# Reordering the passes of the last stage of a backward kernel, and thinning one DMA queue before it

## The chip, the cores and the metric

The kernel runs on one core of one Trainium2 chip. The metric is the device time of one execution in microseconds (us); the profile's span is the part of it that the hardware profiler records.

## What is computed

The reference is the forward pass and the whole backward pass of a block with sequence length S = 2048, width D = 576, H = 32 heads of 128 and a hidden width F = 4608, in bf16:

```python
xn = _layernorm(x, axis=-1)
s = _A_ref(xn, A_k_cache, A_v_cache, A_wq, A_wo)   # attention over the given K and V, projected by wo
g = _silu(_B_ref(xn, B_w_gate, B_w_up, B_w_down))  # (sigmoid(xn Wg) * (xn Wu)) Wd
return x + s * g
...
_out, _vjp = jax.vjp(_f, A_x, A_k_cache, A_v_cache, A_wq, A_wo, B_w_gate, B_w_up, B_w_down)
_grads = _vjp(grad_out)
```

There are nine outputs: the result and eight gradients. What matters here is the gradient of the normalised input, dxn = du Wu^T + dg Wg^T + dQ Wq^T, from which the layernorm's backward pass makes dx (`out_1`), and the gradients dK and dV (`out_2`, `out_3`).

## The kernel before

The kernel goes through stages one after the other: layernorm with the gate and up products, the down product, the attention heads one by one (about two thirds of the time), the output product, the gradients of the hidden layer, then the two stages that matter here. Intermediates that don't fit on the chip go to DRAM and come back: du and dg (`du_d`, `dg_d`, 2048 x 4608), dQ (`dq2_d`) and the heads' outputs (`on2_d`), both 2048 x 4096.

**Turns.** For 23 of the heads dK and dV are computed transposed and lie in `dkT_d` and `dvT_d`. The helper `turn` (L152 to L160) brings one such tile back with a transposing DMA (L157) and, on its next call, stores the tile that the call before has loaded (L160). Each of the 46 turns is 0.5 MB in and 0.5 MB out. Calls are strewn over the last three stages. Each stage has two buffers for them.

**The dW_o and dW_q stage** (L990 to L1056) runs over NHG = 8 groups of 4 heads. A group forms 4 products for dW_o (L1025) and then the products for dW_q (L1036, L1045) from two loaded tiles, `onb` and `dqb` (L1011, L1012), each double buffered. Along the way groups load W_u^T and W_g^T, transposed by the DMA, into `wuT_sb` and `wgT_sb` (L1054). A group calls `turn` twice: behind its first product (L1028) and at its end (L1055). A last call after the loop only stores (L1056).

**The last stage** (L1058 to L1122) runs over NSB = 8 blocks of 256 rows. A block has eight passes that all add to the same four accumulators (two tiles of 128 rows, each split into 512 and 64 columns): three over du with `wuT_sb`, three over dg with `wgT_sb`, each 12 hidden tiles of 128 deep, and two over dQ with `wqT`, each 16 tiles deep. A pass first loads its chunk of du, dg or dQ by a transposing DMA (L1083), 128 x 12 x 256 or 128 x 16 x 256 elements, into one of three buffers (`cf0` to `cf2`) or one of two (`cq0`, `cq1`); a buffer can be loaded anew only when the pass that reads it has ended. W_q^T comes in four quarters of five transposing DMAs each (L92), issued behind the loads of passes 1, 3, 4 and 6 of block 0. The first dQ pass needs quarters 0 and 1, the second quarters 2 and 3. Blocks 1 to 6 call `turn` behind the loads of passes 1 and 5. After its last pass a block's accumulators are drained by ScalarE (L1102), VectorE does the layernorm's backward pass (L1107 to L1119), and dx is stored (L1120).

**What sets the order.** Every DMA with `nc.sync` is issued by SyncE (SP), which keeps the order of the program text (the `manual_schedule` of both stages lists SP). So a load waits until everything ahead of it in SP's queue has been issued, and an entry that waits for a buffer or for a landing holds up all entries behind it. The tiles of the last stage lie where the dW_o stage's tiles were: `cf0` where the dQ tile of even groups was (last used by group 6), `cf2` partly where that of the last group was.

Of the kernel before, what the change touches and what calls it, by code (L numbers as in the profile page):

```python
# [9 lines left out]
bf = mybir.dt.bfloat16  # L10
f32 = mybir.dt.float32
PSUM = bass.MemoryType.PSUM
DRAM = bass.MemoryType.DRAM
P = 128
# [81 lines left out]
def kernel(  # L96
# [6 lines left out]
    nc = tc.nc  # L103
    cfg = dict(cfg or {})
    _, S, D = A_x.shape
    _, H, Sk, Dh = A_k_cache.shape
# [4 lines left out]
    FT = F // P  # L111
    dts = ktiles(D)
    DT = len(dts)
    ncs = ktiles(D, 512)
# [37 lines left out]
    def turn(pool, load=True):  # L152
        old, turned[:] = list(turned), []
        if load and turns:
            src, dst = turns.pop(0)
            t_ = pool.tile([P, NT, P], bf, name="turn")
            nc.sync.dma_start_transpose(t_[:], src)  # L157
            turned.append((dst, t_[:]))
        for (dst, t_) in old:
            nc.sync.dma_start(dst, t_)  # L160
# [30 lines left out]
    with tc.tile_pool(name="pa", bufs=1) as pa:  # L191
# [159 lines left out]
        if True:  # L351
# [9 lines left out]
            with tc.tile_pool(name="a2h", bufs=1, reuse_waits="tile") as hp, \  # L361
# [12 lines left out]
                for sg in range(NT // SG):  # L374
# [7 lines left out]
                    for sl in range(SG):  # L382
# [426 lines left out]
    if True:  # L809
# [19 lines left out]
        with tc.tile_pool(name="c1b", bufs=1, side="right", reuse_waits="tile") as blk, \  # L829
# [29 lines left out]
            for st in range(NT):  # L859
# [9 lines left out]
                accs = [ps.tile([P, 512], f32, name=f"acc{j}") for j in range(len(ncs))]  # L869
# [119 lines left out]
        NHG = H // HG  # L989
        with tc.tile_pool(name="c2b", bufs=1, reuse_waits="tile") as blk, tc.tile_pool(name="c2s", bufs=2, reuse_waits="tile") as sb, \  # L990
# [26 lines left out]
            for hg in range(NHG):  # L1017
                cols = slice(hg * HG * P, (hg + 1) * HG * P)
                onb, dqb = held.pop(hg)
                for hl in range(HG):  # L1020
                    h = hg * HG + hl
                    accs = [ps.tile([P, 512], f32, name=f"acc{j}") for j in range(len(ncs))]
                    for st in range(NT):
                        for j, (n0, nn) in enumerate(ncs):
                            nc.tensor.matmul(accs[j][:, :nn], lhsT=onb[:, st, hl * P:(hl + 1) * P], rhs=ds_all[:, st, n0:n0 + nn],  # L1025
                                             start=(st == 0), stop=(st == NT - 1))
                    if hl == 0:
                        turn(tkp)  # L1028
# [23 lines left out]
                load_hg(hg + 2)  # L1052
                for (dst, src, d0, kd) in wT_loads[2 * hg:2 * hg + 2]:
                    nc.sync.dma_start_transpose(dst[:, :, d0:d0 + kd], src[d0:d0 + kd, :])  # L1054
                turn(tkp)  # L1055
            turn(tkp, False)  # L1056

        SB2 = min(256, S)  # L1058
        FC = ldiv(FT, 12)
        HC = ldiv(H, 16)  # L1060
        with tc.tile_pool(name="c4c", bufs=1, reuse_waits="tile") as chp, tc.tile_pool(name="c4s", bufs=2, reuse_waits="tile") as sb, \
# [11 lines left out]
            for sbi in range(S // SB2):  # L1073
                scol = slice(sbi * SB2, (sbi + 1) * SB2)
                nsl = SB2 // P
                accs = [[ps.tile([P, 512], f32, name=f"acc{sl}_{j}") for j in range(len(ncs))] for sl in range(nsl)]
                passes = []
                for (src_d, wT, nK, KC, nm) in ((du_d, wuT_sb, FT, FC, "cu"), (dg_d, wgT_sb, FT, FC, "cg"), (dq2_d, None, H, HC, "cq")):
                    for k0 in range(0, nK, KC):
                        passes.append((src_d, wT, k0, KC, nm))  # L1080
                for pi, (src_d, wT, k0, KC, nm) in enumerate(passes):
                    ch = chp.tile([P, KC, SB2], bf, name=f"cq{pi % 2}" if nm == "cq" else f"cf{pi % 3}")
                    nc.sync.dma_start_transpose(ch[:], src_d[scol, k0 * P:(k0 + KC) * P])  # L1083
                    if sbi == 0 and pi in (1, 3, 4, 6):
                        load_wqT((1, 3, 4, 6).index(pi))
                    elif sbi and sbi < NSB - 1 and pi % 4 == 1:
                        turn(tkp)
                    last = pi == len(passes) - 1
                    for kk, sl in ([(kk, sl) for sl in range(nsl) for kk in range(KC)] if last else
                                   [(kk, sl) for kk in range(KC) for sl in range(nsl)]):  # L1090
                        k_ = k0 + kk
                        w_ = wT[:, k_, :] if wT is not None else wqT_q[k_ // HQ][:, k_ % HQ, :]
                        for j, (n0, nn) in enumerate(ncs):
                            nc.tensor.matmul(accs[sl][j][:, :nn], lhsT=ch[:, kk, sl * P:(sl + 1) * P], rhs=w_[:, n0:n0 + nn],  # L1094
                                             start=(pi == 0 and kk == 0), stop=(last and kk == KC - 1))
                for sl in range(nsl):
                    st = sbi * nsl + sl
                    rows = slice(st * P, (st + 1) * P)
# [19 lines left out]
                    dx = sb.tile([P, D], bf, name="dx")  # L1118
                    nc.vector.tensor_tensor(dx[:], t2[:], got[:], op=ALU.add)  # L1119
                    (nc.sync if sbi == NSB - 1 else nc.gpsimd).dma_start(o1[rows, :], dx[:])  # L1120
            turn(tkp, False)
            assert not turns  # L1122
        pc3.release()
# [31 lines left out]
```

## Time and profile before

| what | us |
|---|---|
| median of three runs | 5089.01 |
| lowest and highest of them | 5059.81, 5113.86 |
| the profiled execution | 5071.54 |
| its span | 5069.6 |
| TensorE (PE) busy in it | 4957.5 |
| SP's waits for PE in the last stage (L1083 for L1094), 35 times | 106.0 |
| PE's waits at L1094 for loads of `cf` and `cq`, all in block 0 | 9.4, 7.1 and 1.4 |

In a timeline a line gives the start and the duration in us, the engine, the line of code, the operation, the tiles (written <- read) and how many instructions were merged; brackets give the idle time of the engine before them and what ended it. SPq lines show the time that SP took to issue a DMA, not the transfer. In a table of stretches the last columns are the granted PE clock (1.00 is full), the busy share of the DMA engines (overlapping packets make it exceed 1) and the GB/s moved. DMA landing times are counted from the start of the issue.

### The profile page before, as it was taken

Reading aid. Unit: us, or ns where it says so; the run is one execution under the profiler, and the core shown is the slowest. Engines: PE = TensorE matmul, PEld = TensorE weight load, DVE = VectorE, ACT = ScalarE, POOL = GpSimd, SP = SyncE. Lnnn points to the kernel's source line nnn. Section 1 sums busy time; section 2 is a strip of 40 time slices with the busy share of each in tenths; the row PEclk is TensorE's granted clock in tenths of the full one; section 3 lists DMA queues with packets and bytes.
Section 4 is the critical chain, followed back from the end, with each engine's and each line's share of the span. In section 5 each row is a group of like instructions: output and inputs, shape, how many; then the busy total and the mean of one; then the engine's idle time right before and its main releaser. Section 6 shows DMA issues by size and latency. Waiting matters only on the chain.

```text
span 5069.6 us, 107980 instructions
## 1 busy us (share of the span) xinstructions
PE 4957.5 (98%) x45968; PEld 3189.0 (63%) x45968; DVE 3098.6 (61%) x4853; ACT 2390.3 (47%) x3035; POOL 1503.9 (30%) x2197
## 2 busy tenths in 40 slices
PE   9998999999999999999999999999899999998999
PEld 3344777777766666666666666666558777654554
DVE  6545878878887888888788788888532222110101
ACT  5523656666665666666566666656302222100000
POOL 4322333333333333333333333332323333211000
PEclk9999999999999999999999999999999999999999
DMA  7876999999999999999999999999999888899996
GB/s 262 275 213 140 204 209 205 205 206 207 209 202 200 209 213 203 212 207 203 203 203 212 208 207 212 202 209 215 221 203 270 229 233 220 244 285 218 191 189 143
DMA packets 2865204, 1077.14 MB, mean 212 GB/s; under 512 B 2672336, under 2 KB 2795216, under 8 KB 2864720
## 3 DMA queue, kind: packets, MB, share of 16 engines
q1 hardware_dynamic: 2779456, 784.45, 86.1%
q0 software_dynamic: 85264, 285.79, 19.5%
q8 instruction: 359, 5.88, 0.5%
q14 instruction: 125, 1.02, 0.1%
HBM read 172.54 MB, written 225.12 MB: 78 GB/s over the span
## 4 chain that ended last, share of the span: by engine, by line
PE 87%; DVE 4%; issue 4%; DMA 3%; POOL 3%; SPq 0%; ACT 0%; DVEq 0%; POOLq 0%; ACTq 0%
PE acc L620 15%; PE acckv L644 11%; PE sp L556 8%; PE acc L1094 8%; PE dp L589 7%; PE accw L967 5%; PE acckv L641 4%; PE accp L513 4%; PE dh L925 3%; PE acc L392 3%; PE accd L943 3%; PE g_ps L295 3%; PE acc L1025 2%; PE u_ps L295 2%; PE acct L520 2%
## 5 line engine op out<-in xcount | busy, mean ns | idle before, releaser
L568 ACT ACTIVATE Pq<-sneg,nm 128x2048 bf16<-128x2048 bf16 x512 | 1025.9, 2004 | 210.2 <-DVE sneg L558 167.4
L592 DVE SCALAR_TENSOR_TENSOR dSq<-dp,delta,Pq 128x1024 bf16<-128x1024 f32 x608 | 771.0, 1281 | 392.4 <-PE dp L589 392.3
L620 PE MATMUL acc<-Kn,dST 128*128 128x128 bf16 x8192 | 954.8, 219 | 11.0 <-DMA dST<-dSq 7.3
L620 PE MATMUL acc<-Vn,PT 128*128 128x128 bf16 x8192 | 957.6, 219 | 3.9 <-DMA PT<-Pq 3.9
L620 PEld LDWEIGHTS <-dST 128*128 128x128 bf16 x8192 | 670.8, 98 | 364.0 <-DMA dST<-dSq 9.9
L620 PEld LDWEIGHTS <-PT 128*128 128x128 bf16 x8192 | 665.4, 98 | 326.9 <-DMA PT<-Pq 4.6
L558 DVE TENSOR_SCALAR_CACHE_REDUCE sneg<-sp,nm 128x1024 bf16<-128x1024 f32 x512 | 656.9, 1283 | 129.7 <-PE sp L556 114.0
L595 ACT ACTIVATE t<-dp,negdelta 128x1024 bf16<-128x1024 f32 x416 | 463.5, 1114 | 509.8 <-PE dp L589 448.3
L558 DVE TENSOR_SCALAR_CACHE_REDUCE sneg<-sp 128x1024 bf16<-128x1024 f32 x512 | 625.0, 1221 | 93.0 <-PE sp L556 53.5
L589 PE MATMUL dp<-VT,dOT 128*128 128x512 bf16 x2048 | 609.9, 379 | 27.2 <-DVE dSq L592 27.2
L556 PE MATMUL sp<-KT,QT 128*128 128x512 bf16 x2048 | 610.5, 380 | 6.6 <-DVE sneg L558 6.2
L644 PE MATMUL acckv<-Pq,dOn 128*128 128x512 bf16 x1472 | 545.5, 380 | 5.8 <-POOL dOn L576 5.8
L644 PE MATMUL acckv<-dSq,Qn 128*128 128x512 bf16 x1472 | 534.7, 380 | 0.0
L599 DVE TENSOR_TENSOR dSq<-t,Pq 128x1024 bf16<-128x1024 bf16 x416 | 304.6, 732 | 0.0
L576 POOL TENSOR_TENSOR dOn<-dOn,rinv_all 128x256 bf16<-128x256 bf16 x256 | 157.2, 614 | 388.8 <-DVE rinv_all L572 321.4
L1107 DVE SCALAR_TENSOR_TENSOR junk<-dxn,xn_all 128x576 f32<-128x576 f32 x16 | 12.1, 758 | 384.0 <-ACT dxn L1102 384.0
L1094 PEld LDWEIGHTS <-cf 128*128 128x128 bf16 x2304 | 146.8, 99 | 156.3 <-DMA cf<-du_d 9.7
L513 PE MATMUL accp<-xnT,wq_h 128*128 128x512 bf16 x640 | 239.8, 385 | 2.7 <-ACT KT L40 1.1
L967 PEld LDWEIGHTS <-xn_all 128*128 128x128 bf16 x2304 | 224.2, 98 | 27.8
L641 PE MATMUL acckv<-dOn,Pq 128*128 128x128 bf16 x2304 | 217.3, 219 | 1.4 <-POOL dOn L576 1.4
L674 POOL TENSOR_TENSOR prod<-ou,dOn 128x512 f32<-128x512 bf16 x128 | 154.7, 1208 | 207.4 <-ACT ou L40 206.6
L641 PE MATMUL acckv<-Qn,dSq 128*128 128x128 bf16 x2304 | 213.9, 219 | 0.0
(188 smaller groups left out, 7497.4 us busy)
## 6 DMA issues: line engine op xcount, KB each, us to landing
out_dram<-turn SPq DMA_DIRECT2D x46, 512.0 KB, 4.5
h_d<-h_row POOLq DMA_DIRECT2D x48, 384.0 KB, 2.8
a_d<-a_row POOLq DMA_DIRECT2D x48, 384.0 KB, 3.4
b_d<-b_row POOLq DMA_DIRECT2D x48, 384.0 KB, 4.5
a_blk<-a_d SPq DMA_DIRECT2D x18, 1024.0 KB, 6.0
b_blk<-b_d SPq DMA_DIRECT2D x18, 1024.0 KB, 21.6
du_d<-du_blk POOLq DMA_DIRECT2D x18, 1024.0 KB, 8.5
dg_d<-dg_blk POOLq DMA_DIRECT2D x18, 1024.0 KB, 11.5
```

Source lines behind the costliest of these rows:

```text
L513: nc.tensor.matmul(acc[:], lhsT=w[:, i, :], rhs=(srcT if i < DL else xnT)[:, i, cs], start=(i == 0), stop=(i == DL))
L556: nc.tensor.matmul(sp[:, c * CH:(c + 1) * CH], lhsT=hs.QT[:, qs], rhs=hs.KT[:, hf * HW_ + c * CH: hf * HW_ + (c + 1) * CH], start=True, st ...
L558: nc.vector.tensor_scalar(sneg[:, hf * HW_:(hf + 1) * HW_], sp[:], -SCALE, None if hf == 0 else nm[:, hf - 1:hf], op0=ALU.mult, op1=ALU.mi ...
L568: nc.scalar.activation(Pq, sneg[:], AF.Exp, bias=nm[:, hf:hf + 1], scale=-1.0, accum_out=hs.rs_all[:, qt:qt + 1])
L589: nc.tensor.matmul(dp[:, c * CH:(c + 1) * CH], lhsT=hs.dOT[:, qs], rhs=hs.VT[:, hf * HW_ + c * CH: hf * HW_ + (c + 1) * CH], start=True, s ...
L592: nc.vector.scalar_tensor_tensor(dSq[:, hsl], dp[:], hs.delta[:, qt:qt + 1], Pq[:, hsl], op0=ALU.subtract, op1=ALU.mult)
L595: nc.scalar.activation(t[:], dp[:], AF.Identity, bias=hs.negdelta[:, qt:qt + 1], scale=1.0)
L620: nc.tensor.matmul(bx.acc[:, j, :], lhsT=T[qt][:, kt, :], rhs=getattr(hs, rhs)[:, kt, :], start=(kt == 0), stop=(kt == NT - 1))
L641: nc.tensor.matmul(bx.acc[i][:, j * P:(j + 1) * P], lhsT=slabs[qt][:, k0 + j * P:k0 + (j + 1) * P], rhs=w, start=(qt == 0 and j == 0), sto ...
L644: nc.tensor.matmul(bx.acc[i][:], lhsT=w, rhs=slabs[qt][:, k0:k0 + CH], start=(qt == 0), stop=(qt == NT - 1))
L967: nc.tensor.matmul(acc[:kd, :FB], lhsT=xn_all[:, st, d0:d0 + kd], rhs=blk_[:, st, :], start=(st == 0), stop=(st == NT - 1))
L1094: nc.tensor.matmul(accs[sl][j][:, :nn], lhsT=ch[:, kk, sl * P:(sl + 1) * P], rhs=w_[:, n0:n0 + nn], start=(pi == 0 and kk == 0), stop=(las ...
```

## The change

In the last group of the dW_o stage the two calls of `turn` load nothing more: the first one only stores what was loaded before, the second one is gone, as is the storing call after the loop.

In the last stage the body of a pass becomes `do_pass` and the drain becomes `finish`, and an explicit list sets the order: the six du and dg passes of block 0, the six of block 1, then the two dQ passes of block 0, the two of block 1, and from block 2 on blocks in their old order. Blocks 0 and 1 thus hold their accumulators at the same time (8 banks, as the pool has two buffers of each). The four quarters of W_q^T are loaded behind passes 3 and 5 of block 0 and passes 1 and 3 of block 1. Block 1 keeps one turn (behind pass 5); blocks from 2 on call `turn` a third time, behind pass 3, until the 46 turns are used up: blocks 2 to 5 have three each, block 6 has one.

```diff
                     if hl == 0:
-                        turn(tkp)
+                        turn(tkp, hg < NHG - 1)
...
-                turn(tkp)
-            turn(tkp, False)
+                if hg < NHG - 1:
+                    turn(tkp)
...
-                    if sbi == 0 and pi in (1, 3, 4, 6):
-                        load_wqT((1, 3, 4, 6).index(pi))
-                    elif sbi and sbi < NSB - 1 and pi % 4 == 1:
-                        turn(tkp)
...
+            def do_pass(sbi, pi):
+                if pi == 0:
+                    accs_[sbi] = [[ps.tile([P, 512], f32, name=f"acc{sl}_{j}") for j in range(len(ncs))] for sl in range(nsl)]
+                accs = accs_[sbi]
+                src_d, wT, k0, KC, nm = passes[pi]
                 scol = slice(sbi * SB2, (sbi + 1) * SB2)
...
+                ch = chp.tile([P, KC, SB2], bf, name=f"cq{pi % 2}" if nm == "cq" else f"cf{pi % 3}")
+                nc.sync.dma_start_transpose(ch[:], src_d[scol, k0 * P:(k0 + KC) * P])
+                if sbi == 0 and pi in (3, 5):
+                    load_wqT((3, 5).index(pi))
+                elif sbi == 1 and pi in (1, 3):
+                    load_wqT(2 + (1, 3).index(pi))
+                elif sbi and sbi < NSB - 1 and (pi % 4 == 1 or (pi == 3 and sbi > 1)):
+                    turn(tkp)
...
+            order_ = [(sbi, pi) for sbi in range(2) for pi in range(NPF)] + [(sbi, pi) for sbi in range(2) for pi in range(NPF, len(passes))]
+            order_ += [(sbi, pi) for sbi in range(2, NSB) for pi in range(len(passes))]
+            for sbi, pi in order_:
+                do_pass(sbi, pi)
+                if pi == len(passes) - 1:
+                    finish(sbi)
             turn(tkp, False)
```

`NPF` is 6, the number of du and dg passes. The matmuls, the copies, the vector operations and the bytes that are moved are the same as before.

More of the change, by code (lines that the diff above doesn't have):

```diff
@@ L1072 @@
             NSB = S // SB2
-            for sbi in range(S // SB2):
-                scol = slice(sbi * SB2, (sbi + 1) * SB2)
[L1075 to L1083, printed above, removed]
-                    if sbi == 0 and pi in (1, 3, 4, 6):
-                        load_wqT((1, 3, 4, 6).index(pi))
-                    elif sbi and sbi < NSB - 1 and pi % 4 == 1:
-                        turn(tkp)
[L1088 to L1095, printed above, removed]
@@ new lines @@
+            nsl = SB2 // P
+            passes = []
+            for (src_d, wT, nK, KC, nm) in ((du_d, wuT_sb, FT, FC, "cu"), (dg_d, wgT_sb, FT, FC, "cg"), (dq2_d, None, H, HC, "cq")):
+                for k0 in range(0, nK, KC):
+                    passes.append((src_d, wT, k0, KC, nm))
+            NPF = 2 * (FT // FC)
+            accs_ = {}
+            def do_pass(sbi, pi):
[3 more added lines that the diff above has]
+                src_d, wT, k0, KC, nm = passes[pi]
+                scol = slice(sbi * SB2, (sbi + 1) * SB2)
+                ch = chp.tile([P, KC, SB2], bf, name=f"cq{pi % 2}" if nm == "cq" else f"cf{pi % 3}")
[6 more added lines that the diff above has]
+                    turn(tkp)
+                last = pi == len(passes) - 1
+                for kk, sl in ([(kk, sl) for sl in range(nsl) for kk in range(KC)] if last else
+                               [(kk, sl) for kk in range(KC) for sl in range(nsl)]):
+                    k_ = k0 + kk
+                    w_ = wT[:, k_, :] if wT is not None else wqT_q[k_ // HQ][:, k_ % HQ, :]
+                    for j, (n0, nn) in enumerate(ncs):
+                        nc.tensor.matmul(accs[sl][j][:, :nn], lhsT=ch[:, kk, sl * P:(sl + 1) * P], rhs=w_[:, n0:n0 + nn],
+                                         start=(pi == 0 and kk == 0), stop=(last and kk == KC - 1))
@@ L1096, with finish @@
+            def finish(sbi):
+                accs = accs_.pop(sbi)
                 for sl in range(nsl):
```

## Prediction

> **What bounds the kernel now.** First the page: TensorE (PE) is busy for nearly the whole span, so only its gaps can be won.
>
> ```profile
> PE 4957.5 (98%) x45968; PEld 3189.0 (63%) x45968; DVE 3098.6 (61%) x4853; ACT 2390.3 (47%) x3035; POOL 1503.9 (30%) x2197
> ```
>
> Second, PE's timeline where the dW_o stage (L1025 to L1045) hands over to the last stage (L1094).
>
> ```profile
> 4628.82 1.94 PE L1045 MATMUL accq<-dqb,xn_all 128*64 128x256 bf16 x32
> 4640.18 20.14 PE L1094 MATMUL acc<-wuT_sb,cf 128*128 128x512 bf16 x144 [9.42 <-DMA cf<-du_d]
> 4660.15 6.04 PE L1094 MATMUL acc<-wgT_sb,cf 128*128 128x512 bf16 x48
> 4666.88 6.05 PE L1094 MATMUL acc<-wgT_sb,cf 128*128 128x512 bf16 x48 [0.68 <-DMA cf<-dg_d]
> 4679.32 7.59 PE L1094 MATMUL acc<-wgT_sb,cf 128*128 128x512 bf16 x48 [6.39 <-DMA cf<-dg_d]
> 4686.75 8.01 PE L1094 MATMUL acc<-wqT,cq 128*128 128x512 bf16 x64
> 4696.19 8.02 PE L1094 MATMUL acc<-wqT,cq 128*128 128x512 bf16 x64 [1.43 <-DMA cq<-dq_d]
> 4704.04 17.80 PE L1094 MATMUL acc<-wuT_sb,cf 128*128 128x512 bf16 x144
> ...
> 4755.00 17.80 PE L1094 MATMUL acc<-wuT_sb,cf 128*128 128x512 bf16 x144
> ```
>
> From 4704.04 on there is no bracket: a block costs 4755.00 - 4704.04 = 50.96 us (a du or dg pass 5.88, a dQ pass 7.84). Block 0 runs from 4630.76 to 4704.04, 73.28 us, 22.3 too many: 17.92 of gaps (9.42 + 0.68 + 6.39 + 1.43), and passes after long gaps that are slow (20.14 against 17.80, 7.59 against 6.05: 3.9). Third, the queue that feeds these passes, SP's timeline:
>
> ```profile
> 4611.16 2.02 SPq L157 DMA_TRANSPOSE turn<-dvT_d  x1
> ...
> 4624.76 2.51 SPq L157 DMA_TRANSPOSE turn<-dvT_d  x1
> 4627.33 3.09 SPq L160 DMA_DIRECT2D out_dram<-turn  x2
> 4630.46 9.89 SPq L1083 DMA_TRANSPOSE cf<-du_d  x2
> 4640.39 6.68 SPq L92 DMA_TRANSPOSE wqT<-in_A_wq_dram  x5
> 4647.17 3.20 SPq L1083 DMA_TRANSPOSE cf<-du_d  x1
> ```
>
> SP issues without a pause from 4630.46 to 4704: 8 block loads and 20 W_q^T pieces in one block's time. SP, in order, is the bound here, with the DMA engines behind it; and the first load, whose buffer lies over the dQ tile of group 6 (PE done with it at 4599), stands behind the last group's turns. Fourth, stretches (the last three columns are granted PE clock, DMA share, GB/s):
>
> ```profile
> 4631.00:4640.00 9.00, 0.00 (x0) 0.00 (x0) 0.00 (x0) 0.21 (x1) 2.18 (x4) 0.71 1.08 220
> 4640.00:4650.00 10.00, 9.82 (x61) 4.66 (x62) 0.00 (x0) 0.00 (x0) 0.00 (x0) 0.75 1.05 201
> ...
> 4704.00:4755.00 51.00, 51.00 (x419) 26.23 (x417) 6.28 (x17) 1.78 (x8) 2.15 (x4) 1.00 0.93 198
> ```
>
> The clock fell after the 9.42 us gap; later blocks keep it at 1.00, but with a DMA share of 0.93 they have little room.
>
> **The change, part by part.** No matmul, copy or byte is added; PE, ACT, DVE and POOL run the same instructions in a new order, SP the same 46 turns.
>
> *Last group turns nothing.* The loads of the last two turns (the rows at 4617.53 and 4624.76) leave. The store of the turn loaded at 4611.16 waits only for its landing, 5.3 us later by the tile's rows: 4616.5; with 0.6 of issue, SP is at cf0 at 4617.1 instead of 4630.46. By its rows cf0 takes 5.2 us to issue and 9.7 to land: 4626.8. cf1 goes out at 4622.3 and lands 7.0 later, 4629.3. PE frees itself at 4630.76, so the 9.42 gap and its slow pass (2.34) go; cover 4 us. The third buffer straddles group 7's dQ tile, so cf2 waits for PE's last L1045, about 4630.9. Accumulator banks hold nothing up: those of block 0 were drained by copies of earlier products of group 7.
>
> *New order.* Now 12 passes of du and dg (70.6 us) run before W_q^T is needed, and 26.7 us of W_q^T issue (4 x 6.68) lie under them. I walk SP's queue with 3.45 us per cf issue (rows 3.2 to 4.0), 6.5 to landing (5.3 to 7.6), 5.1 and 8.2 for cq, and a buffer free when its pass ends. Issue, landing, PE's need:
>
> - block 0: cf2 4630.9, 4637.4, need 4642.6; pass 3 4636.7, 4643.2, need 4648.5; W_q^T quarter to 4646.8; pass 4 4646.9, 4653.4, need 4654.4; pass 5 4650.3, 4656.8, need 4660.3; quarter to 4660.4.
> - block 1: pass 0 4660.4, 4666.9, need 4666.0, **stall 0.9**; pass 1 in time; quarter to 4674.0; pass 2 4674.0, 4680.5, need 4678.7, **1.8**; pass 3 in time; quarter to 4687.6; pass 4 4687.6, 4694.1, need 4692.3, **1.8**; pass 5 in time; a turn to 4697.7.
> - dQ passes: block 0's land at 4705.9 and 4711.0, in time. Block 1's first has no buffer until PE ends block 0's first at 4713.8, so it lands at 4722.0 for a need of 4721.6, **0.4**; its second lands at 4729.8 as needed.
>
> So both blocks end at 4737.7; 4755.00 before: **-17.3**. New stalls sum to 4.9. With the light rows (3.2, 5.8, cq 4.9 and 7.6) the walk gives 2.4, with the heaviest (4.0, 7.5, cq 6.0 and 9.0, W_q^T 1.5 a piece) 15.8; I take the middle, as the walk set on the old order reproduces its stalls (17.3 against 17.92 of gaps). Bytes agree: block 0's 8 loads and W_q^T, 11.5 MB, took 65.7 us (4630.46 to 4696.1), 175 GB/s; 17.3 MB from 4630.8 at that pace land at 4729.7.
>
> On the clock: gaps of 9.42 and 6.39 us slowed the next pass, 0.68 and 1.43 did not, so stalls below 2 us get no clock cost. The Trainium skill ("TensorE: Matmul & The Clock Gate", HAM oscillation) sets the limit at gaps of about 3.4 us; the trace brackets that, and by it too the walk's stalls cost nothing beyond themselves.
>
> *Third turn in blocks 2 to 5.* The displaced turns (two of the last group, one of block 1) come back there as a load and a store after pass 3; block 6 is left with one turn. SP: 3.1 us more in a block in which it waits for PE for 106.0/7, about 15 us (its waits on L1094): free. DMA: such a block moves 9.6 MB (189 GB/s over the stretch 4704 to 4900, x 50.96) plus 1.05 = 10.7 MB, 209 GB/s, above the 198 of the saturated 4630 to 4705, though a third of it is plain copies, which in the dW_o stage ran in a mix of 279. With 8.4 MB of transposes at 196 and 2.2 MB plain at 350 (estimates: the saturated stretch without its 1 MB of plain copies, and the dW_o stage's best slices of some 360) it needs 49.0 of 50.96 us: it fits, barely. I take 0; if transposes go at 182 the excess is 1.3 x 4 = 5.2. It can't gain, as PE has no gap there.
>
> *End.* Before, a turn's store is issued at 5065.52, behind the dx stores, landing 2.7 later (5068.2); the dx stores land 1.8 after about 5065.3. After, the last turn is stored in block 6: **-1.2** (0 to 2.2, SP's final wait for that store).
>
> **Sum:** -17.3 - 1.2 = -18.5 (at worst -6.5 - 0 + 5.2, at best -19.9 - 2.2). The profiled execution took 5071.54 (span 5069.6 and 1.9 around it): 5053.0. It is 17.5 below the median of the three runs (5059.81, 5089.01, 5113.86); as such spread, not the change, decides the level, I put the sum on the mean of all four executions, 5083.6: **5065**.
>
> **Rivals** (times on the same mean).
>
> 1. The early load does not come early: the cf0 transpose meets the turn's store and group 7's outputs in the queue and lands after PE is done by as much as before. The 9.7 us row already has such company, which speaks against it. Then 9.42 + 2.34 stay: -6.7, 5077.
> 2. No new stalls: SP's 3.4 us per load is backpressure and shrinks once loads are spread. For it: the range down to 3.2 and landings of 5.3. Against: 175 GB/s held for 65 us, and W_q^T pieces at 1.3 us each time. Whole excess gone: -22.3 - 1.2 = -23.5, 5060. The Trainium skill ("DMA: Bandwidth & Descriptors", Latency and other measured facts) gives DMA transposes 261 GB/s and more; this stage's rows reach 198 to 220, and by 261 this rival would hold and the time be 5060.
> 3. Slower: the third turn queues ahead of the first dQ load of each of blocks 2 to 5. That load has the least slack: issued 4728.09, landed 9.0 later, needed 4739.32, so 2.2. A turn costs the queue 4.7 to land and 4.0 to store, 8.7 if nothing overlaps: 6.5 a block, 26 in all, net +7.5, 5091. It decides from 18.5/4 = 4.6 us a block on. Against: the turn is issued after pass 3, some 12 us ahead of that load, and SP then waits for PE, so the queue can drain.
>
> **How the numbers follow.** Forecast 0.72, rival 1 0.08, rival 2 0.12, rival 3 0.08. About 1% (51 us) is what a measurement can tell from no change, and the runs before differ by that. No case reaches it: the gain is 0.36%, and the excess to be won is 0.44%. Faster by over 1% needs the forecast or rival 2 with some 30 us of favourable spread: 0.07; slower needs rival 3 with the opposite: 0.03; within 1% 0.90. The range is the best sum on the fastest run, 5059.8 - 23.5 = 5036, to the forecast on the slowest, 5113.9 - 18.5 = 5095, and holds all rivals' sums.
>
> **What the changed profile would show.** cf0's issue near 4617 and PE passing from L1045 to the last stage without a bracket; the clock at 1.00 there; four short brackets, at block 1's passes 0, 2, 4 and its first dQ pass; block 2 starting some 107 us after L1045's end (102 if rival 2, 119 if rival 1); blocks 2 to 7 at 50.96; no turn store at the end. Brackets at L1094 in blocks 2 to 5 would make it wrong by rival 3; a long one at the stage's start, by rival 1.

## The result, and the profile after

| what | before, us | after, us |
|---|---|---|
| median of 18 runs each | 5081.98 | 5063.58 |
| lowest and highest | 5059.81, 5113.86 | 5046.27, 5087.45 |
| ratio after to before, 95% interval | | 0.9969 (0.9956 to 0.9982) |
| span of the profiled execution | 5069.6 | 5067.4 |
| end of the last L1045 product (its start + 1.94) | 4630.76 | 4643.02 |
| from there to block 2's first matmul ("the stretch") | 124.24 | 110.98 |
| from there to the end of the span ("the tail") | 438.84 | 424.38 |

The change makes the kernel faster by 0.31% of 5081.98, 15.7 us (9.1 to 22.4); the two medians differ by 18.4, inside that interval. The two spans hardly differ, and must not be read as the gain: in the profile of after, the stages ahead of the hand-over, whose code is the same, took 12.3 us longer (4643.02 against 4630.76; a second profile of the same kernel, after_again below, has 4630.60). From the same event on, the end of the last product of the dW_o and dW_q stage, the tail is 14.5 us shorter: 13.3 in the stretch that holds blocks 0 and 1, 1.35 at the kernel's end, and 0.15 lost in blocks 2 to 7 (306.08 from block 2's start to PE's last matmul, against 305.93).

Line numbers move with the change: the matmuls of the last stage are at L1101, its loads at L1088, the drain at L1112. First, the page's line of busy times. Some of PE's records are missing from this trace (45178 matmuls for 45968 weight loads), so PE's sum is not compared, and counts below can be 141 where 144 ran.

```profile
PE 4914.0 (97%) x45178; PEld 3188.2 (63%) x45968; DVE 3098.3 (61%) x4853; ACT 2390.4 (47%) x3035; POOL 1504.2 (30%) x2197
```

Second, PE's timeline at the hand-over, after:

```profile
4641.08 1.94 PE L1045 MATMUL accq<-dqb,xn_all 128*64 128x256 bf16 x32
4642.95 17.81 PE L1101 MATMUL acc<-wuT_sb,cf 128*128 128x512 bf16 x141
4660.60 17.80 PE L1101 MATMUL acc<-wgT_sb,cf 128*128 128x512 bf16 x141
4680.22 11.93 PE L1101 MATMUL acc<-wuT_sb,cf 128*128 128x512 bf16 x94 [1.82 <-DMA cf<-du_d]
4695.28 6.05 PE L1101 MATMUL acc<-wuT_sb,cf 128*128 128x512 bf16 x47 [3.12 <-DMA cf<-du_d]
4701.17 6.04 PE L1101 MATMUL acc<-wgT_sb,cf 128*128 128x512 bf16 x47
4709.20 13.61 PE L1101 MATMUL acc<-wgT_sb,cf 128*128 128x512 bf16 x94 [1.99 <-DMA cf<-dg_d]
4722.64 31.52 PE L1101 MATMUL acc<-wqT,cq 128*128 128x512 bf16 x251
4754.00 17.80 PE L1101 MATMUL acc<-wuT_sb,cf 128*128 128x512 bf16 x141
```

PE goes from L1045 into block 0 without a bracket, and block 0's six passes have none. Brackets stand ahead of block 1's passes 0, 2 and 4, and the passes behind the last of them take 13.61 instead of 11.93. The four dQ passes run as one.

Third, SP's queue. The last group's two turns load nothing, so `cf0` is issued at 4631.17, 11.85 us before the last product ends, where before had 0.30.

```profile
4626.15 2.03 SPq L157 DMA_TRANSPOSE turn<-dvT_d  x1
4628.22 2.85 SPq L160 DMA_DIRECT2D out_dram<-turn  x2
4631.17 15.42 SPq L1088 DMA_TRANSPOSE cf<-du_d  x3
4649.03 3.83 SPq L1088 DMA_TRANSPOSE cf<-dg_d  x1
4652.90 6.68 SPq L92 DMA_TRANSPOSE wqT<-in_A_wq_dram  x5
4659.67 7.04 SPq L1088 DMA_TRANSPOSE cf<-dg_d  x2
4666.76 7.67 SPq L92 DMA_TRANSPOSE wqT<-in_A_wq_dram  x5
4674.53 6.74 SPq L1088 DMA_TRANSPOSE cf<-du_d  x2
4681.32 7.73 SPq L92 DMA_TRANSPOSE wqT<-in_A_wq_dram  x5
4689.15 3.53 SPq L1088 DMA_TRANSPOSE cf<-du_d  x1
```

From 4649.03 on SP issues with hardly a pause until block 1's loads are out. The load that ends the 3.12 us gap is the one at 4689.15: a quarter of W_q^T, 7.73 us of SP's time, stands right ahead of it. The trace names "DMA cf" as what ended the gap; what made that DMA late is read from this queue.

Fourth, stretches (the last three columns are granted PE clock, DMA share, GB/s):

```profile
4709.00:4723.00 14.00, 13.69 (x97) 6.84 (x100) 0.00 (x0) 0.00 (x0) 0.00 (x0) 0.88 1.13 220
4754.00:4805.00 51.00, 50.58 (x409) 26.17 (x416) 6.19 (x17) 1.78 (x8) 2.15 (x4) 1.00 1.11 228
4805.00:4856.00 51.00, 50.53 (x409) 26.21 (x416) 6.33 (x17) 1.78 (x8) 2.15 (x4) 1.00 1.03 211
```

Blocks 2 and 3, with their third turn, move 228 and 211 GB/s at a clock of 1.00 and have no bracket, and take 51.11 and 50.96 us. In after_again block 2 does have one, ahead of its first dQ pass, and the blocks from 2 on take 307.04 us in place of 305.93:

```profile
4776.93 15.86 PE L1101 MATMUL acc<-wqT,cq 128*128 128x512 bf16 x128 [0.76 <-DMA cq<-dq_d]
```

Neither profile of the kernel before has a bracket in these blocks. In after the same place shows only in the weight load, which waited 0.3 us there.

### The profile page after: what moved, and what is told of

It reads as the page before. It is cut to its first block, busy times and chain, and to the rows that moved or that the text cites. A ratio compares the mean times of both kernels' runs of the same rounds, so it can differ in the third digit from the quotient of the medians.

```text
span 5067.4 us, 107190 instructions
## 1 busy us (share of the span) xinstructions
PE 4914.0 (97%) x45178; PEld 3188.2 (63%) x45968; DVE 3098.3 (61%) x4853; ACT 2390.4 (47%) x3035; POOL 1504.2 (30%) x2197
## 4 chain that ended last, share of the span: by engine, by line
PE 84%; DVE 5%; issue 4%; DMA 3%; POOL 3%; SPq 0%; ACT 0%; DVEq 0%; POOLq 0%; ACTq 0%
PE acc L620 16%; PE acckv L644 9%; PE acc L1101 7%; PE sp L556 7%; PE dp L589 6%; PE accw L967 5%; PE acckv L641 5%; PE accp L513 4%; PE dh L925 3%; PE acc L392 3%; PE accd L943 3%; PE g_ps L295 2%; PE acc L1025 2%; PE u_ps L295 2%; PE acct L520 2%
## 5 line engine op out<-in xcount | busy, mean ns | idle before, releaser
L620 PEld LDWEIGHTS <-dST 128*128 128x128 bf16 x8192 | 670.9, 98 | 363.9 <-DMA dST<-dSq 10.7
L589 PE MATMUL dp<-VT,dOT 128*128 128x512 bf16 x1943 | 587.1, 379 | 26.4 <-DVE dSq L592 26.2
L556 PE MATMUL sp<-KT,QT 128*128 128x512 bf16 x1922 | 583.2, 380 | 7.3 <-DVE sneg L558 6.5
L644 PE MATMUL acckv<-Pq,dOn 128*128 128x512 bf16 x1312 | 487.5, 380 | 5.8 <-POOL dOn L576 5.8
L644 PE MATMUL acckv<-dSq,Qn 128*128 128x512 bf16 x1355 | 490.2, 380 | 1.2
L1101 PEld LDWEIGHTS <-cf 128*128 128x128 bf16 x2304 | 145.8, 98 | 145.6 <-DMA cf<-du_d 5.6
L513 PE MATMUL accp<-xnT,wq_h 128*128 128x512 bf16 x609 | 227.8, 384 | 4.4 <-ACT KT L40 1.1
```

What stands on the lines that cost most here:

```text
L513: nc.tensor.matmul(acc[:], lhsT=w[:, i, :], rhs=(srcT if i < DL else xnT)[:, i, cs], start=(i == 0), stop=(i == DL))
L556: nc.tensor.matmul(sp[:, c * CH:(c + 1) * CH], lhsT=hs.QT[:, qs], rhs=hs.KT[:, hf * HW_ + c * CH: hf * HW_ + (c + 1) * CH], start=True, st ...
L589: nc.tensor.matmul(dp[:, c * CH:(c + 1) * CH], lhsT=hs.dOT[:, qs], rhs=hs.VT[:, hf * HW_ + c * CH: hf * HW_ + (c + 1) * CH], start=True, s ...
L620: nc.tensor.matmul(bx.acc[:, j, :], lhsT=T[qt][:, kt, :], rhs=getattr(hs, rhs)[:, kt, :], start=(kt == 0), stop=(kt == NT - 1))
L644: nc.tensor.matmul(bx.acc[i][:], lhsT=w, rhs=slabs[qt][:, k0:k0 + CH], start=(qt == 0), stop=(qt == NT - 1))
```

## The experiments

The question is which limit the stretch hangs on, and which part of the change moved it. Theory A: SP's queue, that is how many entries stand ahead of a block load and how long SP takes to issue them. Theory B: the new order of the passes is what counts, by moving the need for W_q^T behind 12 passes. Theory C: the DMA engines, which can't bring the bytes in time, so that SP's long issues are only their backpressure. Whole times vary by tens of us from run to run, so the stretch of a profiled execution carries most verdicts; its floor, by the matmuls alone, is two blocks of 50.96, 101.92 us.

| kernel | `cf0` issued ahead of the last product's end | gaps | stretch | tail | whole time, ratio to before (interval) |
|---|---|---|---|---|---|
| before | 0.30 | 17.92 | 124.24 | 438.84 | 5081.98 |
| before_again | 2.18 | 14.19 | 121.60 | 436.25 | 5078.61, one run |
| after | 11.85 | 6.93 | 110.98 | 424.38 | 5063.58, 0.9969 (0.9956 to 0.9982) |
| after_again | 14.30 | 5.89 | 109.95 | 424.30 | 5056.83, one run |
| thin_only | 17.59 | 5.66 | 111.22 | 424.43 | 5056.61, 0.9962 (0.9950 to 0.9974) |
| order_only | 4.00 | 9.05 | 114.62 | 427.89 | 5072.61, 0.9990 (0.9976 to 1.0004) |
| order_only_again | 5.77 | 7.50 | 109.94 | 423.19 | 5058.90, one run |
| one_quarter | 15.20 | 0.22 | 102.26 | 416.17 | 5043.59, one run |
| pool_copies | 14.39 | 12.51 | 118.41 | 431.68 | 5074.16, one run |
| sp_tiny | 11.88 | 12.18 | 118.90 | 431.99 | 5063.35, one run |
| five_turns | 12.75 | 4.58 | 108.64 | 439.50 | 5088.60, 1.0021 (1.0004 to 1.0037) |
| early_wq | 26.36 | 0 | 101.86 | 416.70 | 5051.55, 0.9954 (0.9942 to 0.9966) |
| early_wq_again | 28.66 | 0 | 101.86 | 416.50 | 5044.33, one run |
| early_wq_old | 26.07 | 0 | 102.09 | 415.33 | 5057.10, 0.9971 (0.9950 to 0.9993) |

Gaps are the brackets on PE in the stretch that name a DMA, summed; brackets of 0.22 that name "issue" (in before_again and sp_tiny) are left out. The ratios are to times of before that were taken together with the kernel of the line: medians of 5081.98 for after, 5078.22 for thin_only, order_only, early_wq and early_wq_old, 5076.13 for five_turns. A single run says little: the one run of before that was taken together with sp_tiny, before_again, order_only_again and early_wq_again took 5065.19. The stretch and the tail come from one profiled execution each. The edits are against after.

**thin_only**: the last group's turns alone. The order of passes and the places of the W_q^T quarters are those of before.

```diff
-                if sbi == 0 and pi in (3, 5):
-                    load_wqT((3, 5).index(pi))
-                elif sbi == 1 and pi in (1, 3):
-                    load_wqT(2 + (1, 3).index(pi))
+                if sbi == 0 and pi in (1, 3, 4, 6):
+                    load_wqT((1, 3, 4, 6).index(pi))
...
-            order_ = [(sbi, pi) for sbi in range(2) for pi in range(NPF)] + [(sbi, pi) for sbi in range(2) for pi in range(NPF, len(passes))]
-            order_ += [(sbi, pi) for sbi in range(2, NSB) for pi in range(len(passes))]
+            order_ = [(sbi, pi) for sbi in range(NSB) for pi in range(len(passes))]
```

> The thinned last group alone: no turn is loaded in group 7 of the dW_o stage, later blocks take a third turn as in the changed kernel, but the passes keep the old order and the quarters of W_q^T stay behind passes 1, 3, 4 and 6 of block 0. Measure: the two blocks, from the end of the last L1045 product to block 2's first matmul, 124.2 us before, 111.0 after, 101.9 without any stall. Theory A (SP's queue, in order, sets when loads are issued): SP gets at cf0 some 12 us earlier and also issues cf1 and the first quarter while PE is still in group 7, so the gap at the start goes and about half of the later ones; the walk gives 6.6 to 8.6 of stalls, with slow passes after them 109 to 112: nearly the whole gain without the new order, ratio about 0.997. Rival B (the order of the passes is what brings the gain, since W_q^T no longer has to arrive within block 0): only the start gap and its slow pass go (11.8) and block 0's other gaps stay whole: 112.5 or more, with gaps of 6 us at the sixth pass.

PE's timeline of thin_only (last product and block 0):

```profile
4618.03 1.94 PE L1045 MATMUL accq<-dqb,xn_all 128*64 128x256 bf16 x32
4619.90 17.81 PE L1099 MATMUL acc<-wuT_sb,cf 128*128 128x512 bf16 x144
4637.55 11.92 PE L1099 MATMUL acc<-wgT_sb,cf 128*128 128x512 bf16 x96
4653.15 7.73 PE L1099 MATMUL acc<-wgT_sb,cf 128*128 128x512 bf16 x48 [3.68 <-DMA cf<-dg_d]
4660.72 8.00 PE L1099 MATMUL acc<-wqT,cq 128*128 128x512 bf16 x64
4670.70 9.69 PE L1099 MATMUL acc<-wqT,cq 128*128 128x512 bf16 x64 [1.98 <-DMA cq<-dq_d]
```

The start gap is gone, the gap ahead of pass 5 is 3.68 where before has 6.39 and before_again 4.58, and the stretch is 111.22, 10.4 to 13.0 below the two profiles of before and as long as after's. So the turns alone bring about what the whole change brings. Nearly all of it is the start: the start gap and the slow pass behind it were 11.8 us in before and 10.0 in before_again, while the rest of the time above the floor of 101.92 is 9.3 here against 10.6 and 9.7. SP's timeline shows a reason for the shorter gap ahead of pass 5:

```profile
4602.38 7.48 SPq L1088 DMA_TRANSPOSE cf<-du_d  x2
4609.91 7.98 SPq L92 DMA_TRANSPOSE wqT<-in_A_wq_dram  x5
4620.00 3.53 SPq L1088 DMA_TRANSPOSE cf<-du_d  x1
```

SP is so early that the first quarter of W_q^T is issued under group 7's products, which end at 4619.97: one of the four quarters is out of block 0's way. `cf0` has a lead of 17.59 us in this profile, more than the 11.85 and 14.30 of after, whose code is the same up to there; how much of the rest of the stretch hangs on that, one profile can't say. The whole time, 0.9962, is that of six runs.

**order_only** and **order_only_again**: the new order and the spread quarters, with the last group's turns as before.

```diff
-                        turn(tkp, hg < NHG - 1)
+                        turn(tkp)
...
-                if hg < NHG - 1:
-                    turn(tkp)
+                turn(tkp)
+            turn(tkp, False)
```

> The new order of the passes and the spread W_q^T loads alone: group 7 of the dW_o stage turns its tiles as before. Theory A: SP reaches cf0 as late as before, so the gap of 9 to 10 us at the start and the slow pass behind it stay (11.8), and block 1 has the short gaps of the changed kernel: 118 to 121 us for the two blocks, a gain of 3 to 6 us, too small for the timed runs. Rival B: the order brings most of the gain, 113 or less.

> The new order and the spread W_q^T loads with the last group's turns left as they were, once more: the stretch was 114.6 us with a gap of 3.99 ahead of block 0. If that gap depends on where SP stands when group 7's products end, and the kernel before has 9.4 for the same queue, it comes out anywhere between 4 and 10 here and the stretch between 114 and 121; if it is fixed by the new order, 4 and 114 to 116 again.

PE's timeline of the first of the two, with the start gap:

```profile
4641.37 1.94 PE L1045 MATMUL accq<-dqb,xn_all 128*64 128x256 bf16 x32
4647.29 19.26 PE L1101 MATMUL acc<-wuT_sb,cf 128*128 128x512 bf16 x144 [3.99 <-DMA cf<-du_d]
```

114.62 and 109.94 us: the first lies between A's and B's ranges, the second outside what either part of its own expectation gave. The stretch comes down to about after's, but only part of that can be put down to the order. The start gap and the slow pass behind it are 5.4 and 2.2 us here, 11.8 and 10.0 in the two profiles of before; the rest above the floor is 7.3 and 5.8, against 10.6 and 9.7. By this account the order does 2.4 to 4.8 us. The account is rough, since a gap at the start also gives SP time to get ahead of PE. With the turns thinned as well the rest is 9.1 in after, 8.0 in after_again and 6.7 in five_turns, against 9.3 in thin_only, so on top of the thinning the order adds 0.2 to 2.6, though thin_only had the longest lead of these. The start gap (3.99, 2.21) is within 0.1 us the 7.9 that `cf0` takes to land less its lead of 4.00 and 5.77; in before and before_again it is 9.7 less 0.30 and 2.18 (9.42, 7.57). Up to `cf0` the program is the same in these four, and from the last turn of group 5 to `cf0` SP took 43.0 and 41.6 us in the befores, 41.0 and 40.4 here (after: 30.0 and 29.6). Those 1 to 2 us, and the 1.8 less to land, are hardly the order's doing: the first entry of SP that the order moves, a quarter of W_q^T behind `cf1`, goes out in before at 4640.39, when `cf0` has just landed (4640.2), and in before_again 0.4 us ahead of that. What else made them is open. The whole time of order_only (0.9990, -5 us, -12 to +2) gained less than its tails (-8 to -16); it would fit a gain of the order's 2.4 to 4.8 alone, but does not prove it.

**before_again** shows that spread for the kernel before.

> The kernel before once more, for the spread of its hand-over: its stretch from the end of the last L1045 product to block 1's end was 124.2 us, 22.3 above the sum of its matmuls, with a gap of 9.42 ahead of block 0 and of 6.39 ahead of its pass 5. Theory A (the gap at the start is the length of SP's queue against the time of group 7's products): both recur within 3 us, the stretch 120 to 127. If the start gap is under 5 us here, a good part of the gain of the change in the stage is chance of one profile.

```profile
4638.41 1.94 PE L1045 MATMUL accq<-dqb,xn_all 128*64 128x256 bf16 x32
4647.92 1.14 PE L1094 MATMUL acc<-wuT_sb,cf 128*128 128x512 bf16 x4 [7.57 <-DMA cf<-du_d]
```

The start gap recurs at 7.57 and the one ahead of pass 5 at 4.58, within the 3 us that were allowed (9.42 and 6.39 in before); the stretch of 121.60 makes the gain in it 10.6 to 14.3 us rather than one number.

**after_again**, the changed kernel once more.

> The changed kernel once more, for the spread between profiles: if the gaps come from the order in SP's queue they recur at the same passes (block 1's 0, 2 and 4) within 1.5 us each, and the two blocks take 108 to 113 us, wherever the stages before end.

Gaps of 2.71, 2.72 and 0.46 at the same three passes (after: 1.82, 3.12, 1.99); their places recur, their lengths wander. The third differs by 1.53 us, just over the 1.5 that were expected.

**one_quarter**: only the first quarter of W_q^T is loaded, and all dQ passes use it. The number of matmuls stays; the product with the other three quarters is left out of the result.

```diff
-            wqT_q = {k: wp.tile([P, HQ, D], bf, name=f"wqT{k}") for k in (1, 2, 3, 0)}
+            wqT_q = {k: wp.tile([P, HQ, D], bf, name=f"wqT{k}") for k in (0,)}
...
-                if sbi == 0 and pi in (3, 5):
-                    load_wqT((3, 5).index(pi))
-                elif sbi == 1 and pi in (1, 3):
-                    load_wqT(2 + (1, 3).index(pi))
+                if sbi == 0 and pi == 3:
+                    load_wqT(0)
+                elif sbi < 2 and pi < 4:
+                    pass
...
-                    w_ = wT[:, k_, :] if wT is not None else wqT_q[k_ // HQ][:, k_ % HQ, :]
+                    w_ = wT[:, k_, :] if wT is not None else wqT_q[0][:, k_ % HQ, :]
```

> The changed kernel with one quarter of W_q^T loaded (behind pass 3 of block 0) and used in place of all four, so that three quarters are left out of loads and result. If the gaps of block 1 come from W_q^T pieces standing ahead of its loads: no gap but perhaps 0.4 at block 1's first dQ pass, 102 to 103 us for the two blocks. If gaps of 1.8 to 3 us stay before block 1's passes 0, 2 and 4, something else delays these loads.

```profile
4719.74 8.01 PE L1101 MATMUL acc<-wqT,cq 128*128 128x512 bf16 x64 [0.22 <-DMA cq<-dq_d]
```

102.26 us, with no gap in the stretch but this one of 0.22: the gaps of after come from the 15 pieces of W_q^T taken out here. Whether by SP's time or by their bytes, this run can't say; the next two can.

**pool_copies**: bytes without SP. GpSimd copies half of each du and dg chunk of blocks 0 and 1 to a scratch tensor, 12 copies of 393 KB.

```diff
+    scr_d = dram.tile([4, P, 1536], bf, name="scr_d")
...
+                if sbi < 2 and pi < NPF:
+                    nc.gpsimd.dma_start(scr_d[pi % 4], ch[:, :KC // 2, :].rearrange("p k s -> p (k s)"))
```

> The changed kernel with 12 extra plain copies, 393 KB each, of the first half of every du and dg chunk of blocks 0 and 1 to a scratch tensor, issued by GpSimd once the chunk has landed: 4.7 MB more for the DMA engines in the stretch in which PE stalls, nothing more for SP to issue. Theory A (SP's issue is the limit): the two blocks stay at 111 within 3 us, and the GB/s of the stretch rise from 182 by some 40. Rival C (the DMA engines' rate is the limit): 4.7 MB more at 200 to 230 GB/s are 20 to 24 us of queue, the stretch grows to 122 us or more.

**sp_tiny**: SP's time without bytes.

```diff
+    scr_d = dram.tile([48, P, 32], bf, name="scr_d")
...
+                if pi < NPF and (0, 3) <= (sbi, pi) < (1, NPF):
+                    for r in range(3):
+                        nc.sync.dma_start(scr_d[(sbi * NPF + pi) * 3 + r], xn_all[:, pi, r * 32:(r + 1) * 32])
```

> The kernel after, with three tiny stores (128 rows of 64 bytes of the normalised input, into a scratch tensor) from SP behind each of nine block loads, from block 0's pass 3 to block 1's pass 5: 27 entries of some 0.4 us of SP's time each, about 10 us, and hardly any bytes (0.2 MB). The stretch from the end of the last L1045 product to block 2 took 111.0 and 110.0 us in the kernel after. Theory A (SP's time to issue is the limit, whatever it issues): the gaps before block 1's passes grow by most of those 10 us, the stretch 118 to 122. Theory C (the DMA engines are the limit, SP's time at a transposing load is mostly waiting for room in them): the tiny entries fall into that time, the stretch 109 to 113.

A part of SP's timeline in sp_tiny, the tiny stores at L1092:

```profile
4669.29 2.97 SPq L1089 DMA_TRANSPOSE cf<-du_d  x1
4672.31 1.52 SPq L1092 DMA_DIRECT2D scr_d<-xn_all  x3
4673.87 7.47 SPq L92 DMA_TRANSPOSE wqT<-in_A_wq_dram  x5
4681.44 3.02 SPq L1089 DMA_TRANSPOSE cf<-du_d  x1
4684.50 1.53 SPq L1092 DMA_DIRECT2D scr_d<-xn_all  x3
```

and the two halves of the stretch, first of sp_tiny, then of pool_copies, then of after (last columns again clock, DMA share, GB/s):

```profile
4629.00:4689.00 60.00, 51.79 (x399) 26.13 (x404) 0.00 (x0) 0.37 (x1) 2.29 (x5) 0.93 0.90 168
4689.00:4748.00 59.00, 53.70 (x422) 27.58 (x430) 8.68 (x23) 2.68 (x12) 2.15 (x4) 0.98 0.90 180
```

```profile
4640.00:4700.00 60.00, 50.93 (x401) 25.67 (x398) 0.00 (x0) 0.37 (x1) 7.25 (x14) 0.96 1.04 222
4700.00:4759.00 59.00, 55.44 (x445) 28.14 (x444) 9.07 (x24) 2.68 (x12) 3.77 (x7) 0.99 0.99 201
```

```profile
4643.00:4698.00 55.00, 49.59 (x400) 25.67 (x408) 0.00 (x0) 0.37 (x1) 2.18 (x4) 1.00 1.02 190
4698.00:4754.00 56.00, 53.59 (x419) 27.36 (x427) 8.99 (x24) 2.67 (x12) 2.15 (x4) 0.97 0.90 174
```

Both lengthen the stretch by as much: sp_tiny to 118.90 (7.9 to 9.0 above the two profiles of after), in A's range, and pool_copies to 118.41 (7.4 to 8.5), between A's range and C's.

In sp_tiny the nine groups of tiny stores took some 13.7 us of SP's time. The stretch got longer while the DMA engines did less: over the whole of it they moved 174 GB/s against 182 in after, at a share of 0.90 against 0.96, and the block loads landed 5.1 to 5.3 us (medians) after their issue, against 6.0 to 6.1. So SP's time is a limit of its own, as A expected. It is not all of it: the nine loads and four quarters that stand between the tiny stores held SP some 3 us less in sp_tiny than in after, so a part of an entry's time is waiting for the DMA engines, as C has it.

In pool_copies the same engines moved 222 GB/s in the first half where after moves 190, part of it plain copies. The added bytes cost all the same, since SP took longer for the same entries: the four quarters 7.61, 8.25, 10.34 and 8.28 us, 34.5 in all, against 28.75 in after. The longest of them:

```profile
4682.22 10.34 SPq L92 DMA_TRANSPOSE wqT<-in_A_wq_dram  x5
```

Another part of the cost belongs to the experiment itself: a scratch copy still reading `cf0` kept SP until 4648.11, some 1.8 us after PE had ended the pass that used it (4646.33). So neither pure theory holds: the bound is SP's queue, and how long an entry holds it depends on the DMA engines' load.

**five_turns**: more bytes in the blocks that had room. Blocks 2 to 5 turn five times each; the added turns bring and store tiles a second time.

```diff
+    turns_all = list(turns)
...
+                elif sbi in (2, 3, 4, 5) and pi in (2, 6):
+                    turns.append(turns_all[pi + sbi])
+                    turn(tkp)
```

> The changed kernel with five turns in each of blocks 2 to 5 in place of three (eight tiles are turned a second time, to the same values). Theory A (SP's issue): 5 turns take 15.5 us of SP, with loads 46 to 47 of a block's 50.96: still no gap, at most 2 us a block. Rival C with the rates of the prediction (transposes 196 GB/s, plain copies 350): a block needs 57 us of the DMA engines, gaps of 6 us in each of the four blocks, 26 us in all, ratio near 1.002.

A stretch over block 3 of five_turns, and a part of block 2 on PE:

```profile
4809.00:4865.00 56.00, 51.60 (x418) 26.21 (x417) 6.23 (x17) 1.79 (x8) 2.15 (x4) 1.00 1.12 232
```

```profile
4793.00 8.02 PE L1105 MATMUL acc<-wqT,cq 128*128 128x512 bf16 x64 [2.07 <-DMA cq<-dq_d]
4801.59 8.01 PE L1105 MATMUL acc<-wqT,cq 128*128 128x512 bf16 x64 [0.58 <-DMA cq<-dq_d]
```

The four blocks took 55.30, 56.06, 55.26 and 54.80 us, 4.4 a block more than 50.96, at 229 to 232 GB/s in each. That is nearer to C's 6 a block than to A's 2, and SP still waited for PE some 8 us a block, so its time was not used up. This points to the transfers as what sets the pace here, but SP's order has its part: entries behind such a wait go out late, and none of the runs separates the two. Three turns a block (206 to 228 GB/s in after) fit but for the 0.76 us of after_again, five don't.

**early_wq** and **early_wq_again**: what A suggests for a better kernel. Groups 6 and 7 turn nothing, two quarters of W_q^T follow `cf1` at once, and the other two are spread; the order is the new one. **early_wq_old** is the same with the blocks in their old order.

```diff
-                        turn(tkp, hg < NHG - 1)
+                        turn(tkp, hg < NHG - 2)
...
-                if hg < NHG - 1:
+                if hg < NHG - 2:
...
-                if sbi == 0 and pi in (3, 5):
-                    load_wqT((3, 5).index(pi))
-                elif sbi == 1 and pi in (1, 3):
-                    load_wqT(2 + (1, 3).index(pi))
+                WQ_AT = {(0, 1): (0, 3), (0, 4): (1,), (1, 1): (2,)}
+                if (sbi, pi) in WQ_AT:
+                    for k in WQ_AT[sbi, pi]:
+                        load_wqT(k)
```

The lines in which early_wq_old differs from early_wq:

```diff
...
+                WQ_AT = {(0, 1): (0, 3), (0, 2): (1,), (0, 6): (2,)}
...
-            order_ = [(sbi, pi) for sbi in range(2) for pi in range(NPF)] + [(sbi, pi) for sbi in range(2) for pi in range(NPF, len(passes))]
-            order_ += [(sbi, pi) for sbi in range(2, NSB) for pi in range(len(passes))]
+            order_ = [(sbi, pi) for sbi in range(NSB) for pi in range(len(passes))]
```

> A candidate: group 6 turns no tile either (two turns more go to block 6), and two quarters of W_q^T, whose places are free since group 6, are loaded right behind cf1, while PE is still in group 7; the other two behind pass 4 of block 0 and pass 1 of block 1; the passes in the new order. Theory A: SP has 13 us of W_q^T issue done before PE ends group 7, and the walk leaves one stall of 0.4: 102 to 104 us for the two blocks, some 7 to 9 below the changed kernel. Rival C (the DMA engines' rate, some 198 GB/s for transposes, is the limit and SP only feels it): the same bytes are moved earlier, also a gain, but the loads of onb and dqb and the outputs of group 7 share the engines, cf0 lands late, and 3 us or more stay.

> The kernel with two groups that turn nothing and all of W_q^T under the dW_o stage and block 0, once more. Theory A (the gaps come from W_q^T pieces in SP's queue among the block loads, and half of them now lie ahead of the last stage): again no gap over 0.3 us from the last L1045 product to block 2, the stretch 101.9 to 102.5. If the earlier run without a gap was luck, gaps of 1 to 3 us at block 1's even passes, 104 to 110.

> The same early W_q^T with the passes in the old order: quarters 0 and 3 behind cf1, quarter 1 behind pass 2 and quarter 2 behind pass 6 of block 0. Theory A: SP's walk gives no stall at all, 102 to 104 us for the two blocks: once SP has room ahead of the stage, the new order is not needed. Rival B: the old order needs W_q^T within block 0, so gaps of several us stay before the dQ passes: 107 or more.

SP's and PE's timelines of early_wq:

```profile
4599.04 10.74 SPq L1088 DMA_TRANSPOSE cf<-du_d  x2
4609.82 15.64 SPq L92 DMA_TRANSPOSE wqT<-in_A_wq_dram  x10
4625.56 4.33 SPq L1088 DMA_TRANSPOSE cf<-du_d  x1
```

```profile
4623.46 1.94 PE L1045 MATMUL accq<-dqb,xn_all 128*64 128x256 bf16 x32
4625.33 17.81 PE L1101 MATMUL acc<-wuT_sb,cf 128*128 128x512 bf16 x144
4642.98 17.80 PE L1101 MATMUL acc<-wgT_sb,cf 128*128 128x512 bf16 x144
4660.61 17.81 PE L1101 MATMUL acc<-wuT_sb,cf 128*128 128x512 bf16 x144
```

Ten of the 20 pieces have been issued when the last product ends (4625.46 against 4625.40), and PE runs from there to block 2 without a bracket: 101.86 us in both profiles, the floor. C's 3 us or more of gaps are not there. early_wq_old reaches 102.09 in the old order, with the shortest tail of all (415.33), so the new order isn't needed for it. early_wq has the lowest ratio, 0.9954 (0.9942 to 0.9966), and its tail is 7.6 to 7.9 us shorter than after's; its interval overlaps after's, so that it beats after is shown by the tails and not by whole times.

## Why the prediction was right, and where its steps were off

The forecast of 5065 stands beside 5063.58, and its chance of 0.90 was on within 1%, which came. Its mechanism held for the first load and for where the new gaps lie; what the new order is worth was too high. Against its own sum of -18.5, the tails give -11.9 to -14.5 (two profiles of each kernel) and the whole times -15.7 (-22.4 to -9.1). That forecast and median agree to 1.4 us is luck: the interval of the gain alone is 13 us wide.

- *Last group turns nothing.* Right: `cf0` at a lead of 11.85 and 14.30 us where 13.7 was forecast, no start gap, clock 1.00, no slow first pass. The cover, forecast as 4 us, was 2.6 in after: that load took 9.2 to land, hardly less than the 9.7 of before, and it was the earlier issue that counted. Rival 1 fell.
- *New order, new stalls.* Three of four places were right: block 1's passes 0, 2 and 4. The fourth, ahead of block 1's first dQ pass, stayed empty in after and after_again. Their size is the step that was off: the excess over the floor was forecast as 4.9 us and measured as 9.1 in after, 8.0 in after_again and 6.7 in five_turns, whose code is the same there; all inside the walk's ends of 2.4 and 15.8, above its middle. In after, 6.9 of the 9.1 are gaps and 1.7 is a slow pass. The gaps are longer because quarters of W_q^T took 6.68, 7.67, 7.73 and 6.67 us of SP's time, where the walk took 6.68 four times, although one of the four in the profile of before took 7.77 (its issue at 4664.61). Counted from the last product's end SP was 0.1 us behind the walk at pass 3, 0.6 after the first quarter, 1.8, 2.8 and 3.0 after the others; 2.0 of the 3.0 are the quarters, the rest the block loads and short pauses between entries. Rival 2, no new stalls, fell by the gaps themselves; sp_tiny shows besides that SP's time at these entries is only in part backpressure.
- *Clock.* "Stalls below 2 us get no clock cost" was read from four gaps of one profile, and fails: a gap of 1.99 in after and one of 1.98 in thin_only were each followed by passes 1.7 us longer. In after that is 1.7 of the 4.2 us by which the excess was under-read.
- *Third turn.* Nearly right at 0: blocks 2 to 7 cost 0.15 more in after and 1.1 in after_again, whose bracket of 0.76 stands where rival 3 put it, ahead of block 2's first dQ pass. Rival 3 fell as a size (it asked for 6.5 a block), not as a mechanism, which shows there and more at five turns. The rates in this part were loose. The 198 GB/s of the first blocks was taken for a saturated queue, when SP was the limit there; 228 GB/s in block 2 and 229 to 232 in five_turns put what this mix can sustain for a block at 230 or a little more. The plain copies are 2.2 of 10.7 MB by the prediction's own terms, a fifth and not a third; and with 350 GB/s for the plain copies the 196 for transposes comes out at 192, the need at 50.0 of 50.96 us.
- *End.* -1.2 forecast, -1.35 measured: PE's last matmul to the span's end is 7.3 us instead of 8.7.
- *What the prediction didn't see.* Of its -17.3, 11.8 are the start and 5.5 what the new order does to the later gaps. thin_only bears out the first part alone. For the second the order would have had to bring the rest above the floor from 10.6 to 4.9 us; it is 9.1, 8.0 and 6.7 with the whole change and 9.3 without the new order. The quarters of W_q^T, spread as in the change, are the cause of the gaps that are left (one_quarter), and early_wq_old removes them in the old order.

The level has a part in that luck: the sum was put on a mean of four executions, 5083.6, and 18 gave a median of 5081.98. The profiled execution alone would have given 5053.

## What to carry to other kernels

When a load is late, read the issuing engine's queue ahead of it, not only the transfer: here a gain of 10 to 13 us in the stretch (thin_only) came from taking two transfers, which nobody waited for, out of the way of one that PE waited for. Moving the same entries to where that engine waits anyway cost 0.15 to 1.1 us here, and can do so only as long as the DMA engines have room, and the room has to be measured in a stretch in which they, and not the queue, are the limit. Measure from the same event in both traces; two spans can hide a gain of 14 us behind 12 us of spread in stages that were not touched.

## What was unexpected of the hardware

- **Gaps of 2 to 4 us and the clock.** After gaps of 1.98, 1.99, 2.25, 2.44, 2.72, 2.74, 3.68, 3.74, 3.99 and 4.08 us the next passes were 1.4 to 1.7 us longer (in after the granted clock was 0.88 over the passes behind the gap of 1.99); after gaps of 1.82, 1.88, 2.00, 2.07, 2.21, 2.39, 2.61, 2.71, 3.09 and 3.12 they were not. Length alone doesn't decide in this range. The Trainium skill ("TensorE: Matmul & The Clock Gate", HAM oscillation) puts the limit at gaps of some 3.4 us; the slow passes after 1.98 to 2.74 us differ from that, and what decides stays open.
- **SP's time for one entry.** A 128 x 12 x 256 transposing load held SP for 3.0 to 3.3 us at the least (sp_tiny), a piece of W_q^T for 1.3 (6.60 for five), a tiny plain store for 0.5; under the load of pool_copies a piece took 2.1 (10.34 for five).
- **The DMA engines in this mix** of transposes and plain copies moved 229 to 232 GB/s in the four blocks of five_turns in which PE waited for loads. The Trainium skill ("DMA: Bandwidth & Descriptors", Latency and other measured facts) gives transposing DMAs 261 GB/s and more; the last stage reached that for a short time, 267 over 16 us in a mix with plain copies (order_only, 4744 to 4760), but not over the length of a block, where five_turns moved up to 240 (51 us, 4833 to 4884).
